# Sparse attention feeding a dense two-layer network: the order of four engines written out up to the first layer, the block means spread between the scores, weights staged whole

## The chip, the cores and the metric

The kernel runs on one core of one Trainium2 chip. The metric is the device time of one execution in microseconds (us), the median of several runs. The core has a matrix engine (TensorE, PE in the profile), a vector engine (VectorE, DVE), a scalar engine (ScalarE, ACT), a general engine (GpSimd, POOL), and a queue engine (SyncE, SP) that issues most transfers. Each engine takes its own instructions in a fixed order; semaphores hold an instruction until what it reads is there or what it overwrites has been read.

## The reference

```python
# attention: B, H, S, D = 4, 8, 768, 64
k_sum = k.reshape(B, H, nb, block, D).max(axis=3)       # block = 32, nb = 24
v_sum = v.reshape(B, H, nb, block, D).mean(axis=3)
scores_l = scale * np.matmul(q, k.transpose(0, 1, 3, 2))
mask_l = np.abs(pos[:, None] - pos[None, :]) < window   # window = 16
scores_s = scale * np.einsum('bhsd,bhnd->bhsn', q, k_sum) + np.log(block)
scores_all = np.concatenate([np.where(mask_l, scores_l, -1e9), scores_s], axis=-1)
a = softmax(scores_all)                                 # sum + 1e-9 below
attn = np.matmul(a, np.concatenate([v, v_sum], axis=2))
# dense network: x is attn as (3072, 512); w_in (512, 2048), w_out (2048, 512)
h = x @ w_in
P = a[0] + a[1] * h + a[2] * h**2 + a[3] * h**3
Q = 1.0 + np.abs(b[0]) * np.abs(h) + np.abs(b[1]) * h**2
out = (P / (Q + 1e-06)) @ w_out
```

Every query sees the keys closer than 16 positions and 24 summary keys, the maxima over blocks of 32. The summary values are the means of the same blocks.

## The kernel before

**Tiles.** The queries are cut into 48 half-tiles of 64 positions with all eight heads, 12 to a batch, numbered jj. Half-tile jj sees 96 keys around it and 24 summaries, 120 in all. Eight half-tiles make the 512 rows of x of one group; there are six groups. Each group goes through 16 steps, one for every 128 columns of the hidden layer (fc). A step has a first product (`moe1`: h, 12 matmuls), the rational function (`gelu`: tiles tq, ta, tu, gh, gl, on ACT and DVE, and one product on POOL), and a second product (`moe2`: po, 12 matmuls), which runs three steps later (LAG = 3). Both products are three matmuls for one, since x, g and the weights are split into a high and a low part. h(g,fc) below is the first product of group g, step fc.

**One half-tile.** `att_a`: 16 small matmuls on PE write the scores (sc), DVE adds the mask and finds the maxima (four custom instructions, written as minima of negated scores, ss and sm), ACT takes four exponentials, DVE the reciprocal of the sum (L201, L202), POOL normalises in four instructions (L204). `att_b`: four transposes on PE (pt, L222), copied out as pts by ACT (L228). `att_c`: 16 small matmuls with the values (av), rounded into the high part xh by ACT (L252) and the low part xl by DVE (L253).

**Summaries.** The maxima of the keys are one DVE reduction for each pair of heads (ks, L128). The means of the values of batches 0 and 1 are six matmuls each with an averaging matrix (vf, L154); the rows of batch 0 are copied by ACT into six value tiles (L159, L161).

**Weights.** Each of the 16 weights (w_in and w_out of one fc) arrives as 64-bit floats, 1 MB, and is turned into a high and a low 32-bit part: ACT rescales the upper words (L298), POOL takes a byte of the lower words (L300), DVE joins the two (L301), ACT rounds the high part (L304), DVE subtracts for the low part (L305). Weights 0 to 7 are loaded whole into a pool of four buffers (wl); weights 8 to 15 in two halves through a pool of two (`stage`, tag st), which key and value transfers and the output rows use too.

**Order.** A scheduler with a model of the engines sets the order of instructions on ACT, DVE and POOL, by priorities (`tc.high_priority`) and the order of the text. From the first layer on, the matmuls on PE keep the order of the text (`chained`). Up to there all five engines are free. The transfers into SP's queue follow `FIRST` (K keys, Q queries, V value windows, W weights, S constants, F and G values for the means). Then come eight half-tiles (group 0), the means in one block (`AVGAT`, `VLAG`), and three weights (NEARLY); the other weights are due five steps ahead of their own (`CVL = 5`), the attention of later half-tiles in the steps of the group before. Two score buffers, two for h (`ps_h`, used for transposes too) and four for po (used for early scores too) lie in PSUM.

## Time and profile before

| | |
|---|---|
| time, median of 3 runs | 709.06 us (707.88 to 712.47) |
| the profiled execution, its own time | 711.97 us |
| its span | 710.0 us |
| PE busy | 679.1 us, 96% |
| DVE busy | 590.8 us, 83% |
| ACT busy | 471.0 us, 66% |
| POOL busy | 298.9 us, 42% |
| mean granted PE clock | 0.971 |
| first layer starts (first h on PE) | 60.08 us |

The span runs from the first to the last instruction of the profiled execution. Where a row names a tile, the numbers of its buffers are left out: wr is the raw weight, wearly and w the split one. `x16` counts instructions, and a bracket tells how long the engine sat idle before the row, and which instruction ended that. A matmul of 32-bit floats that isn't split shows as two records. "Busy" is a share over stages that are bound by different things, so each stage has to be read by itself. The transfers keep the queues full up to about 50 us, at 272 to 368 GB/s in the page's slices.

### The profile page before, as it was taken

Reading aid. Unit: us, or ns where it says so; the run is one execution under the profiler, and the core shown is the slowest. Engines: PE = TensorE matmul, PEld = TensorE weight load, DVE = VectorE, ACT = ScalarE, POOL = GpSimd, SP = SyncE. Lnnn points to the kernel's source line nnn. Section 1 sums busy time; section 2 is a strip of 40 time slices with the busy share of each in tenths; the row PEclk is TensorE's granted clock in tenths of the full one; section 3 lists DMA queues with packets and bytes.
Section 4 is the critical chain, followed back from the end, with each engine's and each line's share of the span. In section 5 each row is a group of like instructions: output and inputs, shape, how many; then the busy total and the mean of one; then the engine's idle time right before and its main releaser. Section 6 shows DMA issues by size and latency. Waiting matters only on the chain.

```text
span 710.0 us, 11957 instructions
## 1 busy us (share of the span) xinstructions
PE 679.1 (96%) x4196; PEld 527.7 (74%) x4196; DVE 590.8 (83%) x1173; ACT 471.0 (66%) x1058; POOL 298.9 (42%) x320
## 2 busy tenths in 40 slices
PE   8978889989999999999999899999999999999997
PEld 5646667766778777778778677777777777888886
DVE  4567988899889988988879988878988878988885
ACT  2796776878676666776666766666766666675563
POOL 0661534665533544633533454443453443232231
PEclk8796998999999999999999999999999999999999
DMA  9991353452034312132114231211221100010001
GB/s 272 368 342 43 95 174 110 142 166 91 30 116 145 97 34 62 30 112 83 30 31 121 81 103 42 62 30 32 59 76 45 60 12 1 0 60 0 1 1 59
DMA packets 30680, 60.76 MB, mean 86 GB/s; under 512 B 3748, under 2 KB 15396, under 8 KB 29596
## 3 DMA queue, kind: packets, MB, share of 16 engines
q1 hardware_dynamic: 29916, 59.54, 26.6%
q8 instruction: 33, 0.54, 0.3%
q10 hardware_dynamic: 576, 0.25, 0.1%
q14 instruction: 27, 0.22, 0.1%
q0 software_dynamic: 128, 0.20, 0.1%
HBM read 53.44 MB, written 6.34 MB: 84 GB/s over the span
## 4 chain that ended last, share of the span: by engine, by line
PE 69%; DMA 10%; DVE 9%; ACT 5%; POOL 4%; issue 2%; SPq 0%; POOLq 0%; DVEq 0%; ACTq 0%
PE po L78 31%; PE h L78 30%; DMA wr<-in_wio_dram 7%; PE sc L78 4%; POOL ss L204 3%; PE av L78 2%; PE pt L222 2%; DVE tq L327 2%; DMA vr<-in_vpad_dram 2%; DVE gh L332 1%; ACT ss L199 1%; DMA vw<-in_vpad_dram 1%; ACT wr L298 1%; POOL gl L335 1%; DVE tu L331 1%
## 5 line engine op out<-in xcount | busy, mean ns | idle before, releaser
L335 POOL TENSOR_TENSOR gl<-tu,ta 128x512 fp32r<-128x512 f32 x96 | 135.9, 1415 | 229.7 <-DVE tu L334 143.0
L204 POOL TENSOR_SCALAR ss<-ss,sm 128x120 f32<-128x120 f32 x192 | 137.0, 730 | 130.0 <-ACT ta L329 99.4
L327 DVE SCALAR_TENSOR_TENSOR tq<-tq,cs,ta 128x512 f32<-128x512 f32 x96 | 113.6, 1184 | 40.5 <-ACT ta L325 39.7
L324 ACT ACTIVATE tq<-h 128x512 f32<-128x512 f32 x96 | 57.2, 596 | 127.9 <-PE h L78 127.9
L78 PE MATMUL po<-wearly,gh 128*128 128x512 f32 x384 | 130.9, 422 | 0.0
L78 PE MATMUL po<-w,gh 128*128 128x512 f32 x384 | 127.6, 413 | 0.0
L328 ACT ACTIVATE ta<-tq,cs 128x512 f32<-128x512 f32 x96 | 69.7, 726 | 56.6 <-DVE tq L327 55.8
L78 PE MATMUL h<-xh,wearly 128*128 128x512 f32 x384 | 98.9, 401 | 1.1 <-ACT xh L252 1.1
L332 DVE SCALAR_TENSOR_TENSOR gh<-tu,cs,ta 128x512 fp32r<-128x512 f32 x96 | 75.6, 788 | 24.1 <-ACT ta L329 17.6
L78 PE MATMUL h<-xh,w 128*128 128x512 f32 x384 | 95.6, 391 | 0.0
L78 PEld LDWEIGHTS h<-xh,wearly 128*128 128x128 f32 x384 | 74.3, 194 | 17.8 <-ACT xh L252 1.3
L78 PEld LDWEIGHTS h<-xh,w 128*128 128x128 f32 x384 | 72.0, 188 | 16.1 <-DVE w L305 0.3
L199 ACT ACTIVATE ss<-ss,sm 128x120 f32<-128x120 f32 x192 | 73.2, 386 | 13.8 <-DVE sm L195 13.0
L78 PEld LDWEIGHTS po<-wearly,gh 128*128 128x128 f32 x384 | 65.8, 193 | 16.7 <-issue 3.4
L78 PEld LDWEIGHTS po<-w,gh 128*128 128x128 f32 x384 | 66.0, 190 | 15.8 <-issue 2.7
L78 PE MATMUL po<-wearly,gl 128*128 128x512 f32 x192 | 76.2, 397 | 0.0
L78 PE MATMUL po<-w,gl 128*128 128x512 f32 x192 | 75.4, 393 | 0.0
L334 DVE SCALAR_TENSOR_TENSOR tu<-tu,cs,tq 128x512 f32<-128x512 f32 x96 | 72.8, 759 | 2.8
L326 ACT ACTIVATE tu<-h,cs 128x512 f32<-128x512 f32 x96 | 75.0, 781 | 0.0
L331 DVE SCALAR_TENSOR_TENSOR tu<-tu,cs,h 128x512 f32<-128x512 f32 x96 | 71.6, 746 | 2.9
L222 PE MATMUL pt<-ident,ss 128*120 128x128 f32 x192 | 53.5, 292 | 18.1 <-POOL ss L204 17.8
L333 DVE SCALAR_TENSOR_TENSOR tq<-tq,gh 128x512 f32<-128x512 f32 x96 | 67.1, 699 | 2.8
(63 smaller groups left out, 1019.6 us busy)
## 6 DMA issues: line engine op xcount, KB each, us to landing
vw<-in_vpad_dram SPq DMA_DIRECT2D x44, 192.0 KB, 2.7
wr<-in_wio_dram SPq DMA_DIRECT2D x8, 1024.0 KB, 12.2
wr<-in_wio_dram SPq DMA_DIRECT2D x16, 512.0 KB, 4.2
kw<-in_kwin_dram SPq DMA_DIRECT2D x40, 192.0 KB, 2.7
out_dram<-o SPq DMA_DIRECT2D x24, 256.0 KB, 2.1
qw<-in_qw_dram SPq DMA_DIRECT2D x40, 128.0 KB, 2.6
kr<-in_kraw_dram SPq DMA_DIRECT2D x12, 384.0 KB, 3.6
vr<-in_vred_dram SPq DMA_DIRECT2D x8, 384.0 KB, 3.4
```

Source lines behind the costliest of these rows:

```text
L78: ins = nc.tensor.matmul(*args, **kw)
L199: nc.scalar.activation(ss[:, pr, :], ss[:, pr, :], AF.Exp, scale=-1.0, bias=sm[:, 0, pr:pr + 1], accum_out=sm[:, 1, pr:pr + 1])
L204: nc.gpsimd.tensor_scalar(ss[:, pr, :], ss[:, pr, :], sm[:, 1, pr:pr + 1], 1.0, op0=ALU.mult, op1=ALU.mult)
L222: ins = nc.tensor.transpose(out=pt[:NK, pr * P:(pr + 1) * P], in_=ss[:, pr, :], identity=ident)
L326: nc.scalar.activation(tu, h, AF.Identity, scale=cs[:, 3:4], bias=cs[:, 2:3])
L327: nc.vector.scalar_tensor_tensor(out=tq, in0=tq, scalar=cs[:, 5:6], in1=ta, op0=ALU.mult, op1=ALU.add)
L328: nc.scalar.activation(ta, tq, AF.Ln, bias=cs[:, 7:8])
L331: nc.vector.scalar_tensor_tensor(out=tu, in0=tu, scalar=cs[:, 1:2], in1=h, op0=ALU.add, op1=ALU.mult)
L332: nc.vector.scalar_tensor_tensor(out=gh, in0=tu, scalar=cs[:, 0:1], in1=ta, op0=ALU.add, op1=ALU.mult)
L333: nc.vector.scalar_tensor_tensor(out=tq, in0=tq, scalar=C1 * SH, in1=gh, op0=ALU.add, op1=ALU.mult)
L334: nc.vector.scalar_tensor_tensor(out=tu, in0=tu, scalar=cs[:, 0:1], in1=tq, op0=ALU.add, op1=ALU.subtract)
L335: nc.gpsimd.tensor_tensor(gl, tu, ta, op=ALU.mult)
```

## The change

Four engines (`pe`, `dve`, `act`, `gps`) are wrapped. While an engine is in the set `strict`, each of its instructions must follow the one before it in the text. All four are strict up to the first layer; after that only PE is. The text up to there is written out as a list, `EARLY`: s are the scores of a half-tile, e the exponentials and normalisation, p or P transposes and copy (P: the copy on DVE), v one of the six means, m the copies of the means, c the product with the values, w and x the two halves of a weight's conversion (`w_join`, `w_round`).

The six means of batch 0 stand in pairs between the scores of half-tiles 3 to 6. Their rows are copied into two tiles by ACT, two by DVE, and from the first of these into four by POOL; two new value tiles lie in the stage pool, so that all eight value windows are loaded at the start. All copies of the transposes of group 0 move from ACT to DVE. The six means of batch 1 move into steps 0 to 2 of the first layer, two a step.

All weights but the last are loaded whole, into four buffers that rotate. The load of weight fc + 4 (from weight 9 on, fc + 3) is issued where weight fc has been rounded. Conversion is due three steps ahead (`CVL = 3`) and not five. The order of the transfers at the start is new too.

```diff
-CVL = 5
+CVL = 3
...
-VLAG = 5
 NWARM = 6
-FIRST = "Q0 K0 K1 V0 K2 K3 Q1 V1 S V2 W0 V3 F W1 V4 W2 G W3 V5"
+FIRST = "K0 Q0 K1 K2 K3 S F Q1 W0 V0 V1 V2 V3 V4 V5 V6 V7 W1 A8 A9 W2 W3 G"
-AVGAT = 4
+EARLY = ("s0 s1 e0 s2 e1 s3 e2 v0 v1 s4 e3 P0 v2 v3 s5 e4 P1 v4 v5 s6 w0 e5 P2 m0 s7 e6 c0 P3 x0 e7 c1 P4 c2 P5 c3 "
...
+    strict = set()
+
+    class Kept:
+
+
+        def __init__(self, engine):
+            self.engine, self.last = engine, None
+
+        def __getattr__(self, name):
+            def call(*args, **kw):
+                traced = nc.cur_bb.bb.instructions
+                n = len(traced)
+                out = getattr(self.engine, name)(*args, **kw)
+                for ins in nc.cur_bb.bb.instructions[n:]:
+                    if ins.engine == out.ins.engine:
+                        if self.last is not None:
+                            tc.add_manual_dep(ins, self.last, ORDERED, reason="order of the text")
+                        if self in strict:
+                            self.last = ins.name
+                return out
+            return call
+
+    pe, dve, act, gps = Kept(nc.tensor), Kept(nc.vector), Kept(nc.scalar), Kept(nc.gpsimd)
...
-    def value_average(bi, av, vt, i):
-        nc.tensor.matmul(av[:NK, :], avg[:, AVGW - NK - 4 * i:AVGW - 4 * i], vt[i], start=(i == 0), stop=(i == len(vt) - 1))
-        if i < len(vt) - 1:
-            return
-        if bi == 0:
-            for i in range(2):
-                nc.scalar.copy(vw[i][NKW:NK, :], av[NKW:NK, :])
-            for t in vres[2:6]:
-                nc.scalar.copy(t[NKW:NK, :], av[NKW:NK, :])
-        else:
-            t = gp.tile([NK, DM], F32, tag="gh", name="vn")
-            nc.scalar.copy(t[NKW:NK, :], av[NKW:NK, :])
-            nc.sync.dma_start(out=vnext, in_=t[NKW:NK, :])
+    def value_average(av, vt, i):
+        pe.matmul(av[:NK, :], avg[:, AVGW - NK - 4 * i:AVGW - 4 * i], vt[i], start=(i == 0), stop=(i == len(vt) - 1))
+
+    def first_means(av):
+        for t in vres[0:2]:
+            act.copy(t[NKW:NK, :], av[NKW:NK, :])
+        for t in vres[2:4]:
+            dve.tensor_copy(t[NKW:NK, :], av[NKW:NK, :])
+        for t in vres[4:]:
+            gps.tensor_copy(t[NKW:NK, :], vw[0][NKW:NK, :])
+
+    def second_means(av):
+        t = pp.tile([NK, DM], F32, tag="p", name="vn")
+        act.copy(t[NKW:NK, :], av[NKW:NK, :])
+        nc.sync.dma_start(out=vnext, in_=t[NKW:NK, :])
...
+        scores(jj, pool, tag, sbuf)
+        softmax(jj)
+
+    def scores(jj, pool=None, tag="a", sbuf=None):
...
+        att[jj] = ss, sm
+
+    def softmax(jj):
+        ss, sm = att[jj]
...
-    def att_b(jj, pool=None, tag="a", sbuf=None):
+    def att_b(jj, pool=None, tag="a", sbuf=None, copy=None):
...
-        nc.scalar.copy(pts, pt[:NK, :].rearrange("k (r q) -> k r q", r=NPAIR))
+        (copy or act.copy)(pts, pt[:NK, :].rearrange("k (r q) -> k r q", r=NPAIR))
...
+    raws = {}
+
     def w_load(fc):
+        kind = F32 if wio.dtype == F32 else I32
+        words = DM if kind == F32 else 2 * DM
+        if fc == NFC - 1:
+            raws[fc] = [(slice(s, s + 1), stage.tile([P, 1, words], kind, tag="st", name=f"wr{fc}_{s}")) for s in range(2)]
+        else:
+            k = fc % NLATE if fc < NFC - NLATE else fc - (NFC - NLATE) + 1
+            raws[fc] = [(slice(0, 2), wl.tile([P, 2, words], kind, tag=f"wl{k}", name=f"wr{fc}"))]
+        for s, raw in raws[fc]:
+            nc.sync.dma_start(out=raw, in_=wio[fc, :, s, :].bitcast(kind))
...
+    def w_join(fc):
+        if wio.dtype == F32:
+            return
...
+    def w_round(fc):
...
+            wlate[fc] = wl.tile([P, 2, 2, DM], F32R, tag=f"wl{fc - (NFC - NLATE)}", name=f"w{fc}")
...
+        for s, raw in raws.pop(fc):
+            w = raw if wio.dtype == F32 else raw.rearrange("p i (n t) -> p i n t", t=2)[:, :, :, 1].bitcast(F32)
+            act.copy(wt[:, 0, s, :], w)
+            dve.tensor_tensor(wt[:, 1, s, :], w, wt[:, 0, s, :], op=ALU.subtract)
+        ahead = fc + NLATE if fc < NFC - 2 * NLATE else fc + NLATE - 1
+        if fc != NFC - 2 * NLATE and ahead < NFC:
+            w_load(ahead)
+
+    def w_split(fc):
+        w_join(fc)
+        w_round(fc)
...
+    vres = vw + [mp.tile([NK, DM], F32, tag=t, name=f"vr{i}") for i, t in enumerate(("ta", "tq", "ta", "tq"))]
+    vlast = stage.tile([NK, 2, DM], F32, tag="st", name="vlast")
+    vres += [vlast[:, 0], vlast[:, 1]]
...
-            first_q(*((0, 2), (2, HPG))[n])
+            first_q(*((0, 4), (4, HPG))[n])
...
-    av = ps_o.tile([P, DM], F32, tag="o", name="vf")
-    done = 0
-    for i in range(HPG + VLAG):
-        if i < HPG:
-            att_a(i, ps_o, "o", (gp, "gl") if i % 2 else (pp, "p"))
-        if 0 <= i - 1 < HPG:
-            for _ in att_b(i - 1, ps_h, "h", (mp, "tu") if (i - 1) % 5 in (1, 3) else (gp, "gh")):
+    strict |= {pe, dve, act, gps}
+    for what in EARLY.split():
+        n = int(what[1:])
+        if what[0] == "s":
+            scores(n, ps_o, "o", (gp, "gl") if n % 2 else (pp, "p"))
+        elif what[0] == "e":
+            softmax(n)
+        elif what[0] in "pP":
+            for _ in att_b(n, ps_h, "h", (mp, "tu") if n % 5 in (1, 3) else (gp, "gh"), dve.tensor_copy if what[0] == "P" else None):
                 pass
-        while i >= AVGAT and done < 6 and done * (VLAG - AVGAT) < (i - AVGAT + 1) * 6:
-            value_average(0, av, fv, done)
-            done += 1
-        if 0 <= i - VLAG < HPG:
-            att_c(i - VLAG)
-            if i - VLAG < 2:
-                load_v(6 + i - VLAG)
-    av = ps_o.tile([P, DM], F32, tag="o", name="vf1")
-    for i in range(6):
-        value_average(1, av, fv1, i)
-    for jj in (HPG, HPG + 1):
-        att_load(jj)
-    for fc in range(NEARLY):
-        w_split(fc, wr.pop(fc) if fc in wr else w_load(fc))
+        elif what[0] == "v":
+            if n == 0:
+                vf = ps_a.tile([P, DM], F32, tag="a", name="vf")
+            value_average(vf, fv, n)
+        elif what[0] == "m":
+            first_means(vf)
+        elif what[0] == "w":
+            w_join(n)
+        elif what[0] == "x":
+            w_round(n)
+        elif what[0] == "W":
+            w_split(n)
+        else:
+            att_c(n)
+    strict -= {dve, act, gps}
...
-        at(max(fc - CVL, 0), lambda fc: w_split(fc, wr.pop(fc) if fc in wr else w_load(fc)), fc)
+        at(max(fc - CVL, 0), w_split, fc)
...
+        if step < LAG:
+            if step == 0:
+                vf = ps_o.tile([P, DM], F32, tag="o", name="vf1")
+            for i in range(2 * step, 2 * step + 2):
+                value_average(vf, fv1, i)
+            if step == LAG - 1:
+                second_means(vf)
```

What the scheduler makes of it, engine by engine (the number behind a name is that of the tile; ss3 belongs to half-tile 3, w7 or wr7 to weight 7, tq0_2 to group 0, step 2). First PE before step 0. Before, the six means of batch 0 stood in one block:

```order
L78 MATMUL sc4_319<-ks0_124,qres_105 64x24
L78 MATMUL sc4_319<-kres_106,qres_105 64x96 x2
L78 MATMUL sc4_319<-ks0_124,qres_105 64x24 x2
L154 MATMUL vf_165<-vf0_0_149,kres_106 120x512 x4
L154 MATMUL vf_165<-vf0_1_151,kres_106 120x512 x2
L222 MATMUL pt2_312<-ident_92,ss2_256 120x128 x4
L78 MATMUL sc5_371<-kres_106,qres_105 64x96 x2
```

Now the first pair stands between the scores of half-tiles 3 and 4:

```order
L88 MATMUL vf_294<-vf0_0_143,kres_106 120x512 x2
L88 MATMUL sc4_297<-kres_106,qres_105 64x96 x2
L88 MATMUL sc4_297<-ks0_124,qres_105 64x24 x2
L88 MATMUL sc4_297<-kres_106,qres_105 64x96 x2
L88 MATMUL sc4_297<-ks0_124,qres_105 64x24 x2
L88 MATMUL sc4_297<-kres_106,qres_105 64x96 x2
L88 MATMUL sc4_297<-ks0_124,qres_105 64x24 x2
L88 MATMUL sc4_297<-kres_106,qres_105 64x96 x2
L88 MATMUL sc4_297<-ks0_124,qres_105 64x24 x2
L88 MATMUL pt0_330<-ident_92,ss0_189 120x128 x4
L88 MATMUL vf_294<-vf0_0_143,kres_106 120x512 x2
L88 MATMUL sc5_339<-kres_106,qres_105 64x96 x2
```

The means moved apart by a tile of scores and four transposes each. Next POOL, around the end of the early half-tiles, before:

```order
L204 TENSOR_SCALAR ss6_442<-ss6_442,sm6_443 128x120 x4
L300 TENSOR_SCALAR wr4_0_654<-wr4_0_654 128x1024
L204 TENSOR_SCALAR ss7_494<-ss7_494,sm7_495 128x120 x4
L300 TENSOR_SCALAR wr5_0_661<-wr5_0_661 128x1024
L300 TENSOR_SCALAR wr6_0_731<-wr6_0_731 128x1024
L300 TENSOR_SCALAR wr7_0_807<-wr7_0_807 128x1024
L335 TENSOR_TENSOR gl0_0_636<-tu0_0_634,ta0_0_632 128x512
L204 TENSOR_SCALAR ss8_711<-ss8_711,sm8_712 128x120 x4
L335 TENSOR_TENSOR gl0_1_688<-tu0_1_686,ta0_1_684 128x512
L204 TENSOR_SCALAR ss9_780<-ss9_780,sm9_781 128x120 x4
L300 TENSOR_SCALAR wr8_0_882<-wr8_0_882 128x512
L335 TENSOR_TENSOR gl0_2_757<-tu0_2_755,ta0_2_753 128x512
```

and now, from the last early half-tile on:

```order
L88 TENSOR_SCALAR ss7_449<-ss7_449,sm7_450 128x120 x4
L88 TENSOR_SCALAR wr1_158<-wr1_158 128x1024
L88 TENSOR_SCALAR wr2_164<-wr2_164 128x1024
L88 TENSOR_SCALAR wr3_166<-wr3_166 128x1024
L88 TENSOR_SCALAR wr4_487<-wr4_487 128x1024
L88 TENSOR_SCALAR wr5_609<-wr5_609 128x1024
L88 TENSOR_SCALAR wr6_616<-wr6_616 128x1024
L88 TENSOR_SCALAR wr7_653<-wr7_653 128x1024
L88 TENSOR_SCALAR wr8_726<-wr8_726 128x1024
L88 TENSOR_SCALAR ss8_701<-ss8_701,sm8_702 128x120 x4
L88 TENSOR_SCALAR wr9_804<-wr9_804 128x1024
L88 TENSOR_TENSOR gl0_0_635<-tu0_0_633,ta0_0_631 128x512
```

Eight weights instead of three now stand between the normalisations of half-tiles 7 and 8. Last DVE, around the first activation (tq0_0). Before:

```order
L253 TENSOR_TENSOR xl0_412<-av5_557,xh0_411 128x4x64
L253 TENSOR_TENSOR xl0_412<-av6_568,xh0_411 128x4x64
L305 TENSOR_TENSOR wearly_103<-wr6_0_731,wearly_103 128x1024
L301 SCALAR_TENSOR_TENSOR wr7_0_807<-wr7_0_807 128x1024
L253 TENSOR_TENSOR xl0_412<-av7_579,xh0_411 128x4x64
L305 TENSOR_TENSOR wearly_103<-wr7_0_807,wearly_103 128x1024
L327 SCALAR_TENSOR_TENSOR tq0_0_633<-tq0_0_633,cs_95,ta0_0_632 128x512
L330 TENSOR_TENSOR tu0_0_634<-tu0_0_634,h0_0_619 128x512
L331 SCALAR_TENSOR_TENSOR tu0_0_634<-tu0_0_634,cs_95,h0_0_619 128x512
L332 SCALAR_TENSOR_TENSOR gh0_0_635<-tu0_0_634,cs_95,ta0_0_632 128x512
```

and now:

```order
L88 TENSOR_TENSOR xl0_466<-av6_585,xh0_465 128x4x64
L88 TENSOR_TENSOR xl0_466<-av7_596,xh0_465 128x4x64
L88 TENSOR_TENSOR wearly_103<-wr1_158,wearly_103 128x1024
L88 SCALAR_TENSOR_TENSOR wr2_164<-wr2_164 128x1024
L88 TENSOR_TENSOR wearly_103<-wr2_164,wearly_103 128x1024
L88 COPY kw0_96<-ks0_124 128x96
L88 COPY kw1_97<-ks0_124 128x96
L88 SCALAR_TENSOR_TENSOR wr3_166<-wr3_166 128x1024
L88 SCALAR_TENSOR_TENSOR wr4_487<-wr4_487 128x1024
L88 SCALAR_TENSOR_TENSOR tq0_0_632<-tq0_0_632,cs_95,ta0_0_631 128x512
L88 TENSOR_TENSOR tu0_0_633<-tu0_0_633,h0_0_618 128x512
L88 SCALAR_TENSOR_TENSOR wr5_609<-wr5_609 128x1024
```

Weights 3 to 7 were done ahead of tq0_0 and now follow it, in part; weights 8 to 15, which were spread over the activations of steps 3 to 14, now all stand ahead of the activation of step 6. From h(1,0) on, PE, DVE, ACT and POOL have the same rows in the same order in both kernels.

134 lines of the change are left out of this document (54 added, 80 removed).

## The prediction

> **What bounds the kernel now.** I read the busy times by stage first, then PE's instructions in order of time, then the waits. In the stage rows the columns are the stretch, its length, the busy time of PE, PE's weight loads, DVE, ACT and POOL, the granted PE clock, the DMA share and GB/s.
>
> ```profile
> 66.80:181.50 114.70, 102.25 (x641) 77.27 (x640) 104.43 (x224) 87.53 (x202) 62.86 (x67) 0.96 0.39 121
> 290.00:400.00 110.00, 110.00 (x715) 87.17 (x713) 95.15 (x188) 73.44 (x172) 44.20 (x49) 1.00 0.23 70
> 627.15:692.43 65.28, 65.28 (x289) 54.05 (x288) 57.79 (x74) 40.33 (x64) 16.57 (x12) 1.00 0.05 17
> 60.08 3.78 PE L78 MATMUL h<-xh,wearly 128*128 128x512 f32 x8 [1.08 <-ACT xh L252]
> 121.06 1.98 PE L78 MATMUL h<-xh,w 128*128 128x512 f32 x8
> 181.48 1.76 PE L78 MATMUL h<-xh,wearly 128*128 128x512 f32 x7
> 329.18 1.09 PE L78 MATMUL h<-xh,wearly 128*128 128x512 f32 x4
> 342.44 0.85 PE L78 MATMUL h<-xh,w 128*128 128x512 f32 x3
> 665.23 1.98 PE L78 MATMUL h<-xh,w 128*128 128x512 f32 x8
> 670.67 1.07 PE L78 MATMUL h<-xh,w 128*128 128x512 f32 x4
> ```
>
> From about 200 us on PE is full: two steps take 13.26 us with half-tile attention in between (329.18 to 342.44), one step without attention 5.44 (665.23 to 670.67), that is 2.72 for each of its two products, and one half-tile costs PE 13.26 - 2 x 5.44 = 2.38. The last row of stages holds twelve such steps: DVE spends 57.79 / 12 = 4.82 on one activation, ACT 40.33 / 12 = 3.36. What can be won lies ahead of h(1,0), the first product of group 1, at 181.48: step 0 starts at 60.08, step 8 at 121.06. From 66.8 to 181.5 DVE is busy 104.4 of 114.7 us, PE 102.3, so both nearly bind there.
>
> ```profile
> POOL wr L300 <- DMA wr<-in_wio_dram: 12.0, 5, 5.8
> POOL wr L300 <- DMA wr<-in_wio_dram: 16.4, 9, 3.8
> 39.68 1.14 POOL L300 TENSOR_SCALAR wr<-wr 128x1024 int32<-128x1024 uint8 x1 [5.78 <-DMA wr<-in_wio_dram]
> 107.85 0.47 PE L222 MATMUL pt<-ident,ss 128*120 128x128 f32 x1 [3.69 <-POOL ss L204]
> ```
>
> The two wait rows are 0 to 60 us and 60 to 200 us (total, times, longest). POOL stands in its order at a weight whose transfer isn't there (5.78 us at 39.68), the normalisations behind it come late, and PE waits for those (3.69 at 107.85).
>
> **What cannot move.** From h(1,0) on, the order of PE, DVE, ACT and POOL is the same row for row in both kernels. I take 710.0 - 181.48 = 528.5 us as fixed and ask only when h(1,0) starts.
>
> **Up to step 0.** PE, clock and the first minima:
>
> ```profile
> 12.61 0.28 DVE L195 CUSTOM_DVE_ANT_0 ss<-sc,mask 128x120 f32<-128x120 f32 x1 [0.15 <-PE sc L78]
> 12.82 0.28 DVE L195 CUSTOM_DVE_ANT_0 ss<-sc,mask 128x120 f32<-128x120 f32 x1
> 15.34 0.56 PE L78 MATMUL sc<-kres,qres 64*64 64x96 f32 x4
> 15.88 0.56 PE L78 MATMUL sc<-kres,qres 64*64 64x96 f32 x4
> 33.81 0.36 PE L78 MATMUL sc<-kres,qres 64*64 64x96 f32 x4
> 34.09 0.36 PE L78 MATMUL sc<-kres,qres 64*64 64x96 f32 x4
> 33.09 0.65 PE L222 MATMUL pt<-ident,ss 128*120 128x128 f32 x4
> 34.75 0.69 PE L78 MATMUL av<-pts,vw 120*64 120x64 f32 x16
> 57.88 1.12 PE L78 MATMUL av<-pts,vw 120*64 120x64 f32 x16 [2.06 <-DVE xl L253]
> 25.78 6.63 PE L154 MATMUL vf<-vf,kres 128*120 128x512 f32 x12
> 39.29 5.41 PE L154 MATMUL vf<-vf,kres 128*120 128x512 f32 x12
> 11.00:12.00 1.00, 0.76 (x8) 0.46 (x8) 0.93 (x2) 0.00 (x0) 0.00 (x0) 0.61 1.10 353
> 15.00:20.00 5.00, 5.00 (x60) 4.45 (x58) 1.73 (x16) 2.10 (x9) 2.07 (x5) 0.50 1.02 313
> 28.00:29.00 1.00, 1.00 (x3) 0.36 (x2) 0.36 (x1) 0.92 (x3) 0.55 (x1) 0.86 0.92 369
> 65.00:66.00 1.00, 1.00 (x4) 0.81 (x3) 0.00 (x0) 0.40 (x1) 0.00 (x0) 0.59 0.00 0
> ```
>
> A tile of scores has four pairs: 4 x 0.54 = 2.15 us at half clock, 4 x 0.28 = 1.1 at full. Four transposes take 0.65, one half-tile's product with the values (av) 0.69 at full clock and 1.12 at half, one mean 5.41 / 6 = 0.9 at full and so 1.8 at half. The clock falls to half at about 11.2 (0.61 over 11 to 12), and rises at about 28.3 and 65.8.
>
> The keys come as early as before, and the first minima start about 12 rather than 12.61, because two small copies stood ahead of them. PE then works strictly through tiles 1 to 3, 6.4 us at half clock, to 18.4, and through two means, 3.6, to 22; by then I take the clock as lifted (the rival below is that it isn't). Tile 4 ends at 23.1. DVE has the reciprocal of half-tile 3 behind the minima of tile 4, so POOL's fourth normalisation starts only at 23.5: this is the wait that the change adds, and the whole chain queues behind it. Each further half-tile is now 1.1 + 0.65 + 1.8 = 3.6 on PE: POOL's fifth starts at 27.2. After that POOL ends last:
>
> ```profile
> 15.79 1.39 POOL L204 TENSOR_SCALAR ss<-ss,sm 128x120 f32<-128x120 f32 x4 [15.34 <-DVE sm L202]
> 40.92 2.46 POOL L204 TENSOR_SCALAR ss<-ss,sm 128x120 f32<-128x120 f32 x4
> L300 POOL TENSOR_SCALAR wr<-wr 128x512 int32<-128x512 uint8 x16 | 13.0, 812 | 17.6 <-DMA wr<-in_wio_dram 16.4 <-PE pt L222 0.6
> L335 POOL TENSOR_TENSOR gl<-tu,ta 128x512 fp32r<-128x512 f32 x96 | 135.9, 1415 | 229.7 <-DVE tu L334 143.0 <-ACT ta L325 33.6 <-ACT tq L324 19.9
> L353 DVE COPY o<-po 128x512 f32<-128x512 f32 x2 | 1.4, 691 | 4.1 <-PE po L78 4.1
> ```
>
> Four normalisations at 1.39 to 2.46, taken as 1.9, are 7.6; the first weight's byte step is 1.14 (the row at 39.68); four copies of the means, new on POOL, have no row. A pass over 512 columns with one operand is 0.81 (L300), with two 1.4 (L335), and a quarter of the cheapest normalisation row is 0.35: I take 0.8, nearest in shape, so 3.2. With about 2 of waiting for half-tile 5's reciprocal this ends at 27.2 + 12 + 2 = 41. Behind it stand the last transposes, DVE's copy of them (0.69 by the output copy, a move from ACT that costs DVE 8 x 0.69 = 5.5 in all), three half-tiles of av and their rounding, some 5: step 0 at 46, 14 us earlier. The transfers cover this: the first 7 MB that it needs were moved by about 25 us at before's own rate of some 310 GB/s, and nothing of POOL's then waits for one.
>
> **Steps 0 to 5.** The gain is spent here. Before had eight weights ready ahead of its first activation; now three are.
>
> ```profile
> L301 DVE SCALAR_TENSOR_TENSOR wr<-wr 128x1024 int32<-128x1024 int32 x8 | 9.8, 1224 | 9.6 <-POOL wr L300 9.6
> L305 DVE TENSOR_TENSOR wearly<-wr,wearly 128x1024 fp32r<-128x1024 f32 x8 | 10.5, 1313 | 4.1 <-ACT wearly L304 4.0
> L298 ACT ACTIVATE wr<-wr 128x1024 f32<-128x1024 f32 x8 | 9.3, 1168 | 4.6 <-DMA wr<-in_wio_dram 3.2 <-POOL ss L204 1.4
> L304 ACT CAST wearly<-wr 128x1024 fp32r<-128x1024 f32 x8 | 9.1, 1140 | 3.4 <-DVE wr L301 3.4
> L195 DVE CUSTOM_DVE_ANT_0 ss<-sc,mask 128x120 f32<-128x120 f32 x192 | 42.2, 272 | 2.6 <-PE sc L78 2.6
> L128 DVE TENSOR_REDUCE ks<-kr 128x24 f32<-128x768 f32 x12 | 11.2, 935 | 0.4 <-DMA kr<-in_kraw_dram 0.4
> ```
>
> One weight costs DVE 1.22 + 1.31 = 2.54 and ACT 1.17 + 1.14 = 2.31, taking turns. The rest of weight 1 and all of weight 2 end about 6 after step 0's start, at 52. In the new order DVE does all thirteen remaining weights before activation 6: 13 x 2.54 = 33.0, six activations at 4.82 = 28.9, four half-tiles at 4 x 0.27 + 0.35 = 1.4 make 5.8, four key maxima 3.7: 71.4 of durations. Neighbouring instructions overlap by about 0.07 (minima of 0.28 start 0.21 apart), some 100 of them: 64. ACT has 13 x 2.31 + 6 x 3.36 and four half-tiles, about 58, in the same stretch, so the two wait for each other; I add 5: DVE is through at 52 + 69 = 121. PE idles meanwhile: h(0,2) must wait until DVE has read h(0,0), and the transposes of half-tile 8 stand on POOL behind the byte steps of weights 3 to 8. The means of batch 1, 5.4 us on PE, fall into these gaps at no cost; on a full PE they would cost that.
>
> **From there to h(1,0).** When DVE has done activation 5, PE is at the second product of step 4 (about 122, after POOL's 1.4). Ahead of h(1,0) are nine second and eight first products, 17 x 2.72 = 46.2, and four and a half half-tiles, 10.7: 57 us at a full PE. h(1,0) starts at 179 instead of 181.5: **2.5 us gained**. Whole weights instead of halves save little; the transfers are in time, since four whole buffers rotate.
>
> The profiled execution took 711.97 (span 710.0), 2.9 above the median of 709.06. It would be 709.5; the median 706.6, say **706.5**. One per cent, 7 us, is about what a measurement here tells from no change.
>
> **The rivals.** *Faster, 697.5.* For it: 28 us of POOL's waits for transfers go, and DVE was idle 10 us after 66.8. With normalisations at 1.39 (2 us less), copies at 0.35 (1.8) and DVE and ACT interleaved without the 5 us, h(1,0) comes at 170, 9 us more. Against: contention between POOL and DVE is in the 2.46 already, and DVE has more work.
>
> *Slower, 720.* The clock stays at half up to step 0. For it: tiles alone filled PE from 15 to 20 us and the clock stayed at 0.50; only the block of six means lifted it (25.78 to 28.3), and that block is now three pairs. Then from 18.4 on six means (10.8), four tiles (8.6), eight sets of transposes at twice 0.65 (10.4) and eight av at 1.12 (9.0) end at 57.2, step 0 starts at 58, 12 later than forecast; with a little of the weights done meanwhile and a slow restart h(1,0) comes at 192. It decides if no pair lifts the clock. Against: 2.5 us of means were enough, and a pair is 3.6.
>
> [...]
>
> *Nothing gained, 709.* Whole buffers don't end the wait: weight 11 stands on SP's queue behind the store of batch 1's means, weight 5 behind key transfers that wait for the last av.
>
> **Chances.** Forecast 0.45, own range 701 to 713 (step 0 two or three us either way, the same in steps 0 to 5); faster rival 0.31; slower 0.20; nothing 0.04. Of the forecast, 0.06 lies beyond 1% below and 0.05 beyond above, of each outer rival 0.03 inside: faster 0.34, same 0.44, slower 0.22. The range takes in both outer rivals: 695 to 720.
>
> **What would show it.** Right: step 0 at 43 to 49; clock 1.0 within the first two pairs of means; DVE over 90% busy from 52 to 120; PE gaps before h(0,2) and half-tile 8's transposes; step 8 no earlier than 121; 57 us from step 4's second product to h(1,0). Wrong: PEclk 0.5 until step 0 (slower rival); step 8 before 115 (faster); any change after h(1,0) beyond a few us would break the fixed term.

## The result and the profile after

The changed kernel takes **719.24 us** (717.76 to 720.98, median of 4 runs) against 709.32 us (707.88 to 712.47) of the kernel before beside it: a ratio of **1.0135**, 95% interval 1.0093 to 1.0177. It is slower by a little over one per cent, where the forecast was 706.5.

The profiled execution of the changed kernel took 719.88 us, its span is 717.8. TensorE's instructions in order of time (start, duration; every helper is recorded as line 88): step 0, step 2, the transposes of half-tiles 8, 10 and 11, the second product of step 4, step 8, and the next group's first product.

```profile
41.21 2.11 PE L88 MATMUL h<-xh,wearly 128*128 128x512 f32 x8 [0.47 <-ACT xh L88]
54.37 3.29 PE L88 MATMUL h<-xh,wearly 128*128 128x512 f32 x8 [2.79 <-DVE tu L88]
68.06 0.47 PE L88 MATMUL pt<-ident,ss 128*120 128x128 f32 x1 [8.15 <-POOL ss L88]
105.15 0.47 PE L88 MATMUL pt<-ident,ss 128*120 128x128 f32 x1 [6.46 <-POOL ss L88]
117.84 0.47 PE L88 MATMUL pt<-ident,ss 128*120 128x128 f32 x1 [3.91 <-POOL ss L88]
127.95 0.73 PE L88 MATMUL po<-wearly,gh 128*128 128x512 f32 x2
130.81 1.98 PE L88 MATMUL h<-xh,w 128*128 128x512 f32 x8
188.14 1.09 PE L88 MATMUL h<-xh,wearly 128*128 128x512 f32 x4
```

Step 0 starts at 41.2 instead of 60.1, 19 us earlier. Step 8 starts at 130.8 instead of 121.1, and h(1,0) at 188.1 instead of 181.5. So the early part won more than forecast, and the steps 0 to 8 lost all of it and 10 us more: they take 89.6 us, before 61.0. From h(1,0) to the end of the span it is 717.8 - 188.1 = 529.7, before 528.5: the change shows nothing there.

Busy times by stage, of the changed kernel and then of the kernel before (stretch, its length, busy PE, PE's weight loads, DVE, ACT, POOL, granted PE clock, DMA share, GB/s). 118.3 is where DVE finishes activation 5 and the last weight in the changed kernel; the second rows end at h(1,0).

```profile
47.00:118.30 71.30, 44.19 (x238) 30.94 (x237) 68.71 (x112) 53.93 (x96) 36.02 (x30) 0.79 0.54 196
118.30:188.14 69.84, 67.97 (x412) 52.93 (x411) 49.17 (x110) 43.09 (x103) 28.37 (x34) 0.94 0.13 39
```

```profile
47.00:118.30 71.30, 56.76 (x384) 42.84 (x379) 58.41 (x113) 49.35 (x104) 31.83 (x37) 0.83 0.38 123
118.30:181.48 63.18, 57.82 (x352) 43.80 (x353) 58.05 (x126) 50.76 (x118) 38.79 (x39) 1.00 0.40 126
```

This is the whole result in four rows. In the changed kernel DVE is full first (68.7 of 71.3 us, weights for much later steps among it) while PE starves (44.2), and then PE is full (68.0 of 69.8) while DVE has gaps (49.2). Before, both are busy in both stretches. The sums over the two rows matter as much: DVE has 117.9 us of work between 47 us and h(1,0) after the change, and 116.5 before. **At 47 us the changed kernel, already past step 0, has as much work left on DVE as the kernel before, which is 13 us short of step 0.** The 6.7 us by which h(1,0) is later are, seen from DVE, 1.4 us more work and 5.3 us more idle time (141.1 - 117.9 = 23.3, before 134.5 - 116.5 = 18.0).

The waits show how it happens. Total, times, longest; the first three rows are 47 us to h(1,0), the last two 0 to 60 and 60 to 200 us.

```profile
PE pt L88 <- POOL ss L88: 22.0, 6, 8.1
PE h L88 <- DVE tu L88: 6.9, 2, 4.2
DVE tq L88 <- ACT ta L88: 15.1, 9, 6.2
POOL wr L88 <- DMA wr<-in_wio_dram: 9.0, 2, 6.3
POOL wr L88 <- DMA wr<-in_wio_dram: 15.3, 4, 6.2
```

PE waits 22 us for GpSimd's normalised scores, where it waited 13.7 before. Ahead of half-tile 8's, GpSimd stands at the byte step of a weight whose transfer is not there (6.11 us at 60.66), and 3.08 us more before a further weight's; ahead of those of half-tiles 10 and 11 it waits for DVE's reciprocals (sm, 2.01 and 4.03 us). Its waits for transfers are not longer in sum than before (24.3 us, before 28.4); one of them now stands where PE needs the scores. Then DVE waits in its turn. ScalarE works in order, and stands 8.47 us at the copy of half-tile 11's transposes (pts), with activation 6 queued behind it.

GpSimd around half-tile 8 and at half-tiles 10 and 11, then that copy, and DVE behind it:

```profile
60.66 1.11 POOL L88 TENSOR_SCALAR wr<-wr 128x1024 int32<-128x1024 uint8 x1 [6.11 <-DMA wr<-in_wio_dram]
64.85 2.38 POOL L88 TENSOR_SCALAR wr<-wr 128x1024 int32<-128x1024 uint8 x1 [3.08 <-DVE ks L88]
67.33 3.60 POOL L88 TENSOR_SCALAR ss<-ss,sm 128x120 f32<-128x120 f32 x4
104.73 1.39 POOL L88 TENSOR_SCALAR ss<-ss,sm 128x120 f32<-128x120 f32 x4 [2.01 <-DVE sm L88]
114.09 5.14 POOL L88 TENSOR_SCALAR ss<-ss,sm 128x120 f32<-128x120 f32 x4 [4.03 <-DVE sm L88]
122.83 0.59 ACT L88 COPY pts<-pt 120x512 f32<-120x512 f32 x1 [8.47 <-PE pt L88]
124.52 0.75 DVE L88 SCALAR_TENSOR_TENSOR tq<-tq,cs,ta 128x512 f32<-128x512 f32 x1 [6.20 <-ACT ta L88]
```

### The profile page after: what moved, and what is told of

It reads as the page before. It is cut to its first block, busy times and chain, and to the rows that moved or that the text cites. A ratio compares the mean times of both kernels' runs of the same rounds, so it can differ in the third digit from the quotient of the medians.

```text
span 717.8 us, 11913 instructions
## 1 busy us (share of the span) xinstructions
PE 675.4 (94%) x4196; PEld 526.6 (73%) x4196; DVE 598.1 (83%) x1169; ACT 463.5 (65%) x1032; POOL 293.0 (41%) x317
## 3 DMA queue, kind: packets, MB, share of 16 engines
q1 hardware_dynamic: 28908, 59.54, 25.4%
## 4 chain that ended last, share of the span: by engine, by line
PE 79%; DVE 7%; ACT 6%; POOL 4%; DMA 2%; issue 2%; SPq 0%; DVEq 0%; POOLq 0%; ACTq 0%
PE po L88 34%; PE h L88 31%; PE sc L88 5%; PE av L88 3%; POOL ss L88 3%; PE pt L88 3%; DMA wr<-in_wio_dram 2%; DVE tq L88 2%; ACT ta L88 1%; DVE tu L88 1%; PE warm L88 1%; ACT wr L88 1%; ACT ss L88 1%; DVE wr L88 1%; POOL wr L88 1%
## 5 line engine op out<-in xcount | busy, mean ns | idle before, releaser
L88 POOL TENSOR_SCALAR ss<-ss,sm 128x120 f32<-128x120 f32 x192 | 132.0, 703 | 133.7 <-ACT ta L88 104.7
L88 PE MATMUL po<-wearly,gh 128*128 128x512 f32 x384 | 133.5, 430 | 0.0
L88 DVE SCALAR_TENSOR_TENSOR gh<-tu,cs,ta 128x512 fp32r<-128x512 f32 x96 | 73.7, 768 | 24.6 <-ACT ta L88 14.5
```

What stands on the lines that cost most here:

```text
L88: out = getattr(self.engine, name)(*args, **kw)
```

## The experiments

Theory A: the conversions of weights 3 to 15 stand so early in VectorE's and GpSimd's order that PE starves in steps 2 to 7. Rivals: B, the low clock in and behind PE's gaps is the cost (in the changed kernel 0.50 from 55 to 58 us, behind the gap of 2.79, and from 62 to 75, in and behind the gap of 8.15); C, the second means moved into steps 0 to 2 are; D, VectorE's sum of work sets the end of the stage, whatever the order and whenever step 0 starts. All ratios are to the kernel before beside the same run, with their 95% interval. The table holds for each profiled execution the start of h(1,0), and DVE's busy and idle time from 47 us to there, from the view by stages. A profiled execution can be a few us off its run's median (paced4's took 709.33 us, the median is 705.37), so small differences between rows of two runs say little.

| run | ratio | h(1,0) | DVE busy | DVE idle |
|---|---|---|---|---|
| kernel before | 1 | 181.5 | 116.5 | 18.0 |
| changed kernel | 1.0135 (1.0093 to 1.0177) | 188.1 | 117.9 | 23.3 |
| early_only | 1.0002 (0.9974 to 1.0030) | 177.8 | 115.1 | 15.7 |
| weights_only | 1.0020 (0.9991 to 1.0049) | 182.1 | 117.8 | 17.3 |
| after_fill | 1.0127 (1.0096 to 1.0157) | 195.7 | 118.2 | 30.5 |
| after_nomeans | 1.0122 (1.0079 to 1.0165) | 192.9 | 121.5 | 24.4 |
| after_pool | 1.0097 (1.0055 to 1.0140) | 190.8 | 118.4 | 25.4 |
| after_tinyjoin | 0.9959 (0.9928 to 0.9991) | 181.3 | 106.8 | 27.5 |
| paced5 | 0.9969 (0.9930 to 1.0008) | 174.4 | 114.0 | 13.5 |
| paced4 | 0.9923 (0.9883 to 0.9962) | 176.4 | 113.5 | 16.0 |
| paced4_tinyjoin | 0.9707 (0.9685 to 0.9729) | 160.5 | 100.4 | 13.1 |
| after_slack | 1.0050 (1.0023 to 1.0077) | 183.6 | 118.7 | 17.9 |
| before_slack | 1.0029 (0.9997 to 1.0060) | 179.9 | 115.7 | 17.1 |
| **paced4_slack** | **0.9865** (0.9818 to 0.9912) | 167.3 | 112.9 | 7.4 |
| **weights_paced_slack** | **0.9865** (0.9828 to 0.9901) | 171.5 | 112.2 | 12.3 |
| paced4_slack_psub | 0.9933 (0.9910 to 0.9955) | 173.5 | 116.7 | 9.8 |

### Each half of the change alone

`early_only`: the changed kernel with the weights as before.

```diff
-CVL = 3
+CVL = 5
...
-    wl = ctx.enter_context(tc.tile_pool(name="wl", bufs=1))
+    wl = ctx.enter_context(tc.tile_pool(name="wl", bufs=NLATE))
...
-        if fc == NFC - 1:
+        if fc >= NSTG:
...
-            w_load(ahead)
...
 def w_split(fc):
+    if fc not in raws:
+        w_load(fc)
     w_join(fc)
     w_round(fc)
```

> The changed kernel with the weights handled as in the kernel before: weights 8 to 15 in two halves through the stage pool, each load issued where its conversion is written, five steps ahead; the early order, the copies of the means and the second means between the steps stay as changed. Theory A (the whole staging lets the conversions of weights 3 to 15 run ahead of scores 8 to 11 and of the activations 2 to 5 on VectorE and GpSimd, and TensorE starves in steps 2 to 7): step 0 stays at 41 us, step 8 comes at 115 to 121 instead of 130.8, the next group's first product at 170 to 178, time 699 to 708. Rival B (the clock lost in the short gaps of steps 1 and 2, and the second means there, are the cost whatever the conversions do): step 8 at 127 or later and 714 to 720. Rival D (VectorE's sum of work from the start of the steps sets the end, in whatever order it is done): the next group's first product at 180 or later as in both kernels, 708 to 714.

`weights_only`: the kernel before, with `w_load`, `w_join`, `w_round` and `w_split` of the changed one, its four buffers, and `CVL = 3`.

```diff
-        w_split(fc, wr.pop(fc) if fc in wr else w_load(fc))
+        w_split(fc)
```

> The kernel before with only the weights handled as changed: whole, in four named buffers, each load issued when the weight four ahead of it is rounded, conversions written three steps ahead; the part up to the first layer as before. Theory A: step 0 at 60 us as before, then the same crowding, step 0 to step 8 80 to 90 us instead of 61, the next group's first product at 190 to 200, time 717 to 730. Rival B (the gaps and the second means of the new early order are the cost): step 0 to step 8 stays at 58 to 66 us, and the time is 702 to 710. Rival D: VectorE has the same sum of work from 60 us on, 706 to 712.

Neither half alone costs or gains anything clear of noise: 710.43 us (ratio 1.0002) and 712.29 (1.0020). Theory A was right that the staging turns the early order into a loss, and wrong that the early order without it gains (699 to 708): step 8 comes at 113.7, 7 us ahead of the kernel before, but h(1,0) at 177.8 only 3.7 us ahead, for a step 0 that is 19 us earlier. And the staging alone does not reach the 717 that A asked for: step 0 to step 8 takes 70 us and not 80 to 90, and DVE idles no longer than before (17.3 us). The loss needs both halves. That it is the pair "little converted at step 0, and the conversions first in the order" is argued here; the orders changed alone, below, test the second part of it. Rival D's times fit the first half and miss the second by 0.3 us; those of A and B miss both.

### The clock, the means, GpSimd's order

In these three the orders of VectorE, ScalarE and the transfers were held row for row as in the changed kernel; in the first two GpSimd's too. `keep_warm(n)` is n products of 128x512 zeros into a free accumulator; the second stands ahead of half-tile 8's transposes.

```diff
+        if step == 1:
+            keep_warm(6)
...
+        if step == 2:
+            keep_warm(16)
```

> The changed kernel, every engine's order held as it is, with 6 idle 512-column products of zeros on TensorE ahead of step 2 and 16 ahead of half-tile 8's transposes, where it waits 2.8 and 8.2 us; they go into an accumulator that is free there. Rival B (the half clock after these gaps is what costs): the clock stays at full from 50 to 75 us, step 3 starts at 69 to 71 instead of 73.9, time 709 to 715. Theories A and D: step 3 may start earlier, but step 8 stays within 2 us of 130.8, time 717 to 721.

The same stretch, changed kernel and then this run (PE alone: busy, clock, DMA share, GB/s):

```profile
60.00:65.00 5.00, 0.00 (x0) 0.67 1.00 395
```

```profile
60.00:65.00 5.00, 5.00 (x32) 1.00 0.91 329
```

PE is busy without a pause and the clock full from 55 to 85 us, and the time does not move (722.42 us, ratio 1.0127). Step 8 comes at 138.4 (step 0 at 45.0), where A and D asked for about 131, and the time is outside B's 709 to 715. But this is no clean test of rival B, because the filler overruns. GpSimd ends half-tile 8's normalisations at 73.70, and the 16 products hold PE until 78.2:

```profile
64.73 13.47 PE L94 MATMUL cold<-zero 128*128 128x512 f32 x31
78.03 0.60 PE L94 MATMUL pt<-ident,ss 128*120 128x128 f32 x4
```

So PE itself kept these transposes back by 4.3 us. ScalarE's copy of them stood 9.94 us (5.83 in the changed kernel) and DVE behind it 6.67 (2.59). What the full clock gives and what the filler takes are not apart here. Rival B as the main cause falls by other runs: `early_only`, `paced5` and `paced4` miss its times, and `after_tinyjoin` (below) is some 12 us faster than the changed kernel at nearly the same low clock (0.89 against 0.87 from 47 us to h(1,0)). What the half clock adds to the loss beside the main cause is not shown.

```diff
-            for i in range(2 * step, 2 * step + 2):
-                value_average(vf, fv1, i)
+            if step == LAG - 1:
+                pe.matmul(vf[:NK, :], avg[:, 0:NK], fv1[0], start=True, stop=True)
```

> The changed kernel, every engine's order held as it is, but five of the six pairs of products for the second means (in the steps 0 to 2) are left out, so that the means are not those wanted; nothing else. It takes some 5 us of TensorE's work out of the first three steps. Rival C (the means moved into the steps are what pushes them): the next group's first product 4 to 6 us earlier, 713 to 716. Theory D with the order: TensorE waits that much longer before half-tile 8's transposes, 717 to 721.

721.87 us, 1.0122: taking 5 us off PE in these steps gains nothing clear of noise, and in the profiled execution step 0 to step 8 still takes 89.1 us (46.5 to 135.6), for 89.6. Rival C falls.

The third moves two things on GpSimd:

```
 byte step of weight 6
+scores of half-tile 8
 byte step of weight 7, byte step of weight 8
-scores of half-tile 8
+scores of half-tile 9
 byte step of weight 9, gl of step 0, byte step of weight 10
-scores of half-tile 9
```

> The changed kernel with the orders of TensorE, VectorE, ScalarE and the transfers held as they are, and two moves on GpSimd alone: the four scalings of the scores of half-tile 8 stand ahead of the byte step of weight 7 instead of behind weight 8's, and those of half-tile 9 ahead of weight 9's instead of behind weight 10's. If GpSimd's queue alone starves TensorE, half-tile 8's transposes start at 60 to 62 instead of 68.1, step 3 at 66 to 69 instead of 73.9, and the next group's first product comes 4 to 6 us earlier: 713 to 716. If VectorE is the engine that all wait for (busy without a pause from 47 to 118 us in its order, weights first), the transposes start earlier but step 8 stays within 2 us of 130.8: 717 to 721.

The first rows of the two places in this run:

```profile
64.95 0.47 PE L94 MATMUL pt<-ident,ss 128*120 128x128 f32 x1 [5.96 <-POOL ss L94]
133.52 0.39 PE L94 MATMUL h<-xh,w 128*128 128x512 f32 x1
```

The transposes of half-tile 8 come 3 us earlier and step 3 (68.9) 5 us earlier, but step 8 comes at 133.5 and h(1,0) at 190.8. The time, 719.67 us (1.0097), has an interval that holds the changed kernel's ratio. The local gain did not reach step 8: the weights pushed back on GpSimd came back as waits of PE for gl (3.78 us at 79.08) and for DVE (4.89 at 89.24).

### The amount of VectorE's work

```diff
+            n = DM if fc < NEARLY else 8
-            dve.scalar_tensor_tensor(out=h32, in0=h32, scalar=3, in1=l32, ...)
+            dve.scalar_tensor_tensor(out=h32[:, :, 0:n], in0=h32[:, :, 0:n], scalar=3, in1=l32[:, :, 0:n], ...)
```

The join of weights 3 to 15 is done on 16 of the 1,024 values of a partition, and the low bits of the others are left out. All orders are held. First in the changed kernel's order:

> The changed kernel, every engine's order held as it is, but VectorE's shift-and-or of weights 3 to 15 is done on 16 of the 1,024 values of a partition: the low bits of the others are left out, all other work is done. That takes some 17 us of VectorE's 118 us between 47 us and the next group's first product. Rival D (VectorE's remaining work sets the end of this stage): the next group's first product moves from 188 to 170 to 176, time 700 to 708. Theory A (the order, conversions on GpSimd and VectorE ahead of the scores' weights, starves TensorE; the amount matters little): gaps before half-tiles 8, 10 and 11 stay within 2 us of 8.1, 6.5 and 3.9, time 712 to 719.

and then in the order of the run `paced4` (below):

> The run with conversions kept behind the activation four steps back, its orders held as they are, with the same 17 us of VectorE's shift-and-or left out (16 of 1,024 values done for weights 3 to 15). Rival D: the next group's first product moves from 176 to 160 to 166, time 689 to 697. Theory A (with the crowding gone, the rest is the latency of the softmax chain in TensorE's fixed order): 700 to 706.

710.56 us (0.9959) and 692.73 us (0.9707). DVE's busy time up to h(1,0) falls by 11 and 13 us (the table), and the time by 1.0135 - 0.9959, or 1.8% (12 to 13 us), and by 0.9923 - 0.9707, or 2.2% (15 us): about one for one in either order by the medians. In the profiled executions h(1,0) comes 6.8 and 15.9 us earlier, so in the changed order some of DVE's saving shows as more idle time. In the paced order that is what D asked for (689 to 697) and not A (700 to 706). In the changed order the time lies between the two forecasts (D to 708, A from 712): PE's gaps stay, as A said (9.0, 4.6 and 3.5 us), and DVE idles 27.5 us, the price of the order. A and D each hold a part: less work on DVE shortens the stage in either order, and the order decides how much is lost on top.

### Conversions kept behind the activations

`paced5`, and `paced4` with 4 in place of 5: the conversion of weight n stands on each engine behind the last instruction of the activation of step n - 5.

```diff
+PACE, PFROM = 5, 3
 def w_split(fc):
+    n = len(traced)
     w_join(fc)
     w_round(fc)
+    if fc >= PFROM and fc - PACE >= 0:
+        for ins in traced[n:]:
+            if ins.engine in marks[fc - PACE]:
+                tc.add_manual_dep(ins, marks[fc - PACE][ins.engine], ORDERED, ...)
```

> The changed kernel with one addition: each engine's conversion instructions of weight n (from 5 on) are kept behind the last instruction of the activation of step n minus 5 on that engine; nothing else. Theory A: VectorE and GpSimd no longer convert weights 6 to 15 ahead of scores 8 to 11 and of the activations, TensorE's gaps before half-tiles 8, 10 and 11 shrink to under 3 us each, step 0 to step 8 takes 62 to 75 us, the next group's first product comes at 166 to 178, time 695 to 708. Rival B: the gaps and the half clock of steps 1 to 3 stay, 712 to 720. Rival D: 708 to 714, with VectorE over 90% busy from 47 us to the next group.

> As the run with five steps, but the conversion of weight n behind the activation of step n minus 4. Theory A: crowding is the least here, but a weight is ready only just before its step: the first steps as with five, and waits of TensorE for a weight's rounding of 1 to 3 us at some of the steps 5 to 15; time 695 to 710, at most 5 us from the run with five. Rival B: 712 to 720. Rival D: 708 to 714.

708.05 us (0.9969) and 705.37 (0.9923): the loss of the changed kernel is undone by an order alone. The first lies on the border of A's and D's times, the second inside A's and outside D's. DVE's idle time falls from 23.3 to 13.5 and 16.0 us, and some 4 us less of DVE's work lies ahead of h(1,0). PE still waits at the transposes (17.0 and 18.3 us for GpSimd's scores between 41 and 175 us, the longest 5.1 and 4.5, where A asked for under 3), so theory A, that the crowding makes these waits, was only half of it.

### The transposes one step later

```diff
+        late = 1 if jj < 2 * HPG else 0
-        at(start_of(jj) + 2, att_c, jj)
+        at(start_of(jj) + 2 + late, att_c, jj)
         at(start_of(jj), half_a, jj)
-        at(start_of(jj) + 1, att_b, jj)
+        at(start_of(jj) + 1 + late, att_b, jj)
```

On top of `paced4`, then on the changed kernel, then on the kernel before:

> The run with conversions kept behind the activation four steps back, and in the first group the transposes and the value products of half-tiles 8 to 15 one step later in TensorE's order. If the waits of TensorE for GpSimd's scaled weights (18 us in all) are a matter of latency, they fall below 6 us and the next group's first product comes at 162 to 168, time 691 to 698. Rival D (VectorE's sum of work sets it and the waits only show it): the waits move to other instructions, and the time is within 4 us of 705.

> The changed kernel with one addition: in the first group the transposes and value products of half-tiles 8 to 15 stand one step later in TensorE's order. The conversions still stand first in VectorE's and GpSimd's order. If TensorE's fixed order is what lets VectorE idle (23 us from 47 us to the next group), the idle time falls to 10 us or less and the next group's first product comes at 172 to 177: 703 to 708. If the conversions' place is the cause, TensorE waits for the activations' results (gl, gh) in the place of the scaled scores, VectorE stays busy on weights to 115 us or later and idles as long behind it: 714 to 720.

> The kernel before with the same one addition, the transposes and value products of half-tiles 8 to 15 one step later. If TensorE's fixed order costs it as much as the changed kernel, its 18 us of idle VectorE fall to 8 to 12 and the next group's first product comes at 171 to 176 instead of 181.5: 700 to 705. If the place of the conversions is the only cause, the kernel before, which spreads them over the steps, gains under 3 us: 706 to 710.

702.34 us (0.9865), 716.27 (1.0050) and 714.26 (1.0029). PE's waits from 47 to 188 us in the first:

```profile
PE pt L89 <- DVE sm L89: 4.2, 1, 4.2
PE h L89 <- DVE tu L89: 4.0, 1, 4.0
PE pt L89 <- ACT x L89: 2.5, 2, 1.3
PE pt L89 <- POOL ss L89: 2.2, 2, 1.4
```

With both remedies the waits for GpSimd's scores all but go, h(1,0) comes where it was expected if the waits were a matter of latency (162 to 168), and DVE idles only 7.4 us, the least of all. The whole time is D's all the same (701 to 709) and not the 691 to 698 expected with latency, since what follows h(1,0) took 532.8 us in this execution. The later transposes alone give the changed kernel 0.85%, and leave it slower than before: PE then stands at the next thing behind a weight (7.0 us for gl at 75.8, 7.9 for DVE at 108.7). They give the kernel before nothing, against both forecasts (700 to 705 and 706 to 710). PE's waits there, from 47 us to h(1,0), sum to 20.0 us, for 19.8 without: those for GpSimd are gone, and others stand in their place, for sm (5.8 us) and xl (5.2) from DVE, and for weights that come in halves and just in time (5.0):

```profile
171.40 3.68 PE L78 MATMUL h<-xh,w 128*128 128x512 f32 x8 [3.43 <-ACT w L304]
```

So the fastest runs with all the work have three things together: whole weights ahead of need, conversions no earlier than the activations allow, and slack at the transposes. Leaving out the second costs 1.9%. Leaving out the third costs 0.6%, which the two intervals don't quite tell from nothing. That the first is needed as well is argued: no run has the other two with weights in halves.

### What the head start of step 0 is worth

`weights_only` with the pacing of the weights from 8 on and the later transposes:

```diff
+PACE, PFROM = 4, 8
+late = 1 if jj < 2 * HPG else 0
```

> The kernel before with the weights handled as changed, the conversions of weights 8 to 15 kept behind the activation four steps back, and the transposes of half-tiles 8 to 15 one step later; the early part as before, so that step 0 comes at 58 to 60 us instead of 40. Rival D (VectorE's work left at 47 us is the same with either early part, so the head start of step 0 is worth little): the next group's first product at 169 to 175, time 699 to 706, within 4 us of the same with the changed early part. If the head start is worth its 18 us once the steps are in good order: 184 to 188, time 714 to 720.

The same three things with the **old** early part give 703.59 us, ratio 0.9865: the same as with the new one. From 47 us to h(1,0), first this run, then `paced4_slack`:

```profile
58.69 3.78 PE L80 MATMUL h<-xh,wearly 128*128 128x512 f32 x8 [1.03 <-ACT xh L254]
47.00:171.50 124.50, 111.19 (x724) 86.37 (x725) 112.17 (x220) 97.96 (x203) 66.83 (x66) 0.90 0.39 131
```

```profile
47.00:167.30 120.30, 104.88 (x643) 78.78 (x641) 112.91 (x218) 95.48 (x195) 72.28 (x64) 0.94 0.41 137
```

Step 0 comes at 58.7 in one and 40.1 in the other, and DVE has 112 to 113 us left in both. The head start of 18.6 us shows as 4.2 us at h(1,0). What follows was longer in the second, 532.8 us against 526.7 (span minus h(1,0)); but this term lies anywhere between 526.6 and 533.6 in the profiled executions here, so that it gives the 4.2 us back is not shown. The intervals of the two ratios leave room for a few us as well. Rival D holds for the early part this far: of 18.6 us, about 4 at most are left.

### VectorE's work moved to GpSimd

```diff
-            dve.tensor_tensor(wt[:, 1, s, :], w, wt[:, 0, s, :], op=ALU.subtract)
+            (gps if fc in (7, 10, 13) else dve).tensor_tensor(wt[:, 1, s, :], w, wt[:, 0, s, :], op=ALU.subtract)
```

> The run with the conversions kept behind the activation four steps back and the transposes one step later, and the difference that gives the low part of weights 7, 10 and 13 on GpSimd instead of VectorE. VectorE loses three instructions of about 1.4 us, 4.2 us in all; GpSimd, 60% busy there, gains three of 2.5 to 4 us. Rival D: 698 to 702 against 702.3 for the run without; if GpSimd's queue is by now as near the path as VectorE, or the two slow each other, 702 to 707.

708.04 us (0.9933), slower than without. DVE's busy time from 47 us to h(1,0) did not fall by 4 us but rose from 112.9 to 116.7, over a stretch that is 6 us longer. Both forecasts (698 to 702, 702 to 707) are missed. The subtractions are gone from DVE's rows, but its other instructions got longer in sum: 216 instructions took 116.7 us in this stretch, and without the move 218 took 112.9, the three subtractions among them.

## Why the prediction was wrong, point by point

**The fixed term held.** 528.5 us was taken from h(1,0) to the end, 529.7 was measured.

**Up to step 0, too slow, chiefly because of the clock.** Step 0 at 46 (43 to 49); it came at 41.2. The four copies of the means on GpSimd took 0.6 us each and not 0.8. The granted clock did not fall at about 11 us at all in this execution: it stayed at 1.00 up to about 31 us and was 0.50 from 31 to 37.6. It rose there under transposes and av alone, so no block of means was needed for it. In an execution with the same instructions up to step 0 where the clock was 0.58 from 10 to 20 us (the last section), step 0 came at 46.5, as forecast. So the slower rival, the half clock up to step 0, is not what happened, although its time, 720, is about the one measured. That is luck: a right number from a mechanism that did not act is no support for it.

**Steps 0 to 5, right in mechanism, and the sum with some luck.** "DVE is through at 52 + 69 = 121": the stretch began at 46.9 and ended at 118.3, 71.4 us for 69, with DVE over 96% busy. Two terms were off the opposite way: 64 us of work came to 68.7 (the twelve whole joins took 1,417 ns each, for 1,224 in the sum), and 5 us of waiting to 2.6. The gaps of PE before h(0,2) and half-tile 8 were there.

**"When DVE has done activation 5, PE is at the second product of step 4 (about 122) ... 57 us at a full PE": this step failed.** At 118.3 PE was still at the second product of step 3, whose first transposes had waited for GpSimd to 117.84; step 4's began at 127.95, and from there to h(1,0) it took 60.2 us. That is 5.9 us later and 3.2 us longer, the 9.1 us by which 188.1 misses 179. The second part is no full PE either: it waited 1.84 us at 136.50 for GpSimd's scores once more, and its clock was 0.87 from 127.95 to 140. The rest of the 12.7 us between 706.5 and 719.2 is the fixed term (1.2) and the difference between the profiled execution and the median, taken as 2.9 us and 0.6 after the change (2.3). What made PE late is a normalisation that began late, behind DVE's reciprocal (4.03 us), and then took 5.14 us itself, for 1.39 at 104.73 (the last section), and an in-order copy on ScalarE behind it, which let DVE idle 6.2 us just when it had caught up. The step counted 1.4 us of GpSimd there and nothing else.

**"The transfers are in time, since four whole buffers rotate": wrong.** A buffer comes free only when its weight has been rounded, the next megabyte then has to come (7.0 us from issue to landing, the median of the fifteen whole weights), and GpSimd stood 6.11 us at 60.66 for it. The rival that the transfers are still late, which got 0.04, had this part right.

**The deeper fault** lies in the form of the sum. It asked when step 0 starts, then when DVE is through, then how long PE needs, one behind the other. It never compared DVE's work left at one and the same time in both kernels. That would have shown that the early order takes nothing off DVE. The first 47 us by stage, and the groups of copies that the change put on DVE (20 to 60 us; count, busy, mean ns), of the changed kernel:

```profile
0.00:47.00 47.00, 41.47 (x462) 28.40 (x463) 30.48 (x114) 25.56 (x83) 20.09 (x45) 0.93 0.98 325
```

```profile
L88 DVE COPY pts<-pt 120x512 f32<-120x512 f32 x7 | 4.7, 678 | 0.4 <-PE pt L88 0.4
L88 DVE COPY vr<-vf 24x512 f32<-24x512 f32 x2 | 1.3, 692 | 0.0
```

and the first 47 us of the kernel before:

```profile
0.00:47.00 47.00, 44.01 (x380) 28.09 (x382) 25.19 (x101) 29.89 (x88) 19.84 (x37) 0.82 1.00 325
```

DVE had worked 30.5 us against 25.2. The 5.3 us more are not even all that the change itself put there: eight copies of transposes and two of means at 0.68 to 0.69 are 6.8 us. No run leaves these copies on ScalarE, so what the early order would be worth without them stays open.

The forecast was right that the gain is spent in the steps, and had it end with 2.5 us left; it was spent whole, and the order cost 5 us more.

## What to carry to other kernels

Where two engines nearly bind, don't count a head start of the one: pick a fixed time, and compare how much work the *other* still has to do from there to the first point where nothing differs, and how much of that it will idle. Work done ahead of need is no gain where it stands in front of what the other engine waits for; two engines that are full one after the other take the sum. Give in-order engines slack at the longest chain (here the transposes), and let the filler work in only behind what feeds them.
